# q of batch 1 transposed by DMA from ScalarE's queue in place of TensorE

## The chip, the cores and the metric

The kernel runs on one core of a Trainium2 chip. The metric is the device time of one execution in microseconds, as a median over executions. Engines are named as in the profile: PE is TensorE, ACT is ScalarE, DVE is VectorE, POOL is GpSimd, SP is SyncE, which in this kernel does nothing but issue DMAs.

## The reference, cut to what matters

```python
batch, n_heads, seq, head_dim = 8, 8, 576, 64          # q, k, v, float32
d_model, d_ff = 512, 1024                              # w1, w2: 512x1024; w3: 1024x1024; w_out: 1024x512

def phi(x):
    return np.where(x > 0, x, np.exp(x) - 1.0) + 1.0

q_p, k_p = phi(q), phi(k)
kv = np.einsum('bhsd,bhse->bhde', k_p, v)
z = np.sum(k_p, axis=2)
num = np.einsum('bhsd,bhde->bhse', q_p, kv)
den = np.einsum('bhsd,bhd->bhs', q_p, z)[..., None] + 1e-06
x = (num / den).transpose(0, 2, 1, 3).reshape(4608, 512)

a, b = x @ w1, x @ w2
out = (a * b @ w3) @ w_out
```

## The kernel before

Every step of the program stands in one table, `ORDER`. A step such as `QP.1.0.a` calls the function `s_QP(1, 0)` with engine letter `a` (ACT; `v` is DVE, `s` SP). The steps are recorded in the order of the table, and each engine runs its own instructions strictly in that order; the framework adds the semaphore waits. So a step's place in the table is its place in the queue of every engine that it uses.

Weights come first. `L3`, `LH`, `LO` load w3 and w_out; `T3` transposes w3 on PE, `FW` multiplies it with w_out, so that the second half of the network is one 1024x512 matrix `wf_sb`. `LA`/`CA` and `LB`/`CB` load w1 and w2 in pieces and cast them to bf16.

The attention works by batch b and by half h of the heads (64 sequence rows of two heads share the 128 partitions). `LK`, `LQ`, `LV` load 576 KB each into one of 13 raw buffers. `EX` takes the exponential on ACT (L263), `PT` makes max(x,0)+1 on DVE (L275), and `PM` the minimum of the two on DVE (L282), which is phi. `VC` casts v (L285). `KV` (or `KB`, both halves) makes kv on PE (L298) and copies it out of PSUM.

For the numerator and the denominator PE needs phi(q) with head_dim on the partitions. Two kinds of step do that. `QP` (L322 to L328) transposes nine 128x128 blocks on PE into a PSUM tile `qp` and copies them to SBUF as `qt`; batches 0 and 1 use it. `QD` (L330) is one DMA with transposition from SP, `phq` to `qt`; batches 2 to 7 use it. Then `ND` (one tile of 128 tokens) or `NT`/`NM` (three tiles) multiply `qt` with kv on PE (L344), divide on DVE and write x as `xn`; `XP` on PE or `XD` by DMA transposes that to `xt`.

The network takes chunks of 512 tokens. `F.c.f` makes one of the eight 128-wide column blocks of chunk c: four matmuls into `a_ps`, four into `b_ps` (L428), a copy `a_sb` from `a_ps` by ACT (L437) and a product into `ab` by DVE (L439). `FP` and `FI` are parts of such steps in the first chunk. `O` multiplies with `wf_sb` (L463), `S` stores. The matmul results `a_ps`, `b_ps`, `o_ps`, `xp` take turns in four PSUM buffers, first free first used, so PE's next group waits until the oldest has been copied out.

The program around the change: `FI`, then `F.0.4` to `F.0.7`, with the preparation of batch 1 between them, `KV.1.0` and `KV.1.1`, `O.0`, then `ND.4`, the first step that reads `qt` of batch 1.

DMA completion is told by eight semaphores, `DMAHW0` to `DMAHW7`, handed out in turn in the order of the table, whichever queue the DMA is on. A DMA on SP waits first until the DMA that had its semaphore last has landed, so up to eight are under way.

Of the kernel before, what the change touches and what calls it, by code (L numbers as in the profile page):

```python
# [9 lines left out]
F32 = mybir.dt.float32  # L10
BF16 = mybir.dt.bfloat16
AF = mybir.ActivationFunctionType
ALU = mybir.AluOpType

P = 128
NCH = 512
# [11 lines left out]
PT.k.0.1 T3.7.1.a LH.0.1 FW.7.0.a FW.7.1.v FW.1.2.v VC.0.0.v QP.0.0.v QP.0.1.a FW.7.2.a KV.0.0.a  # L28
PM.k.0.1 VC.0.1.v FW.7.3.v FW.1.3.a KV.0.1.v T3.0.1.a ND.0 FW.0.0.v LA.6 ND.1 FW.0.1.v CA.6.a LA.7
CA.7.a ND.2 FW.0.2.a XP.0.a XP.1.a ND.3 FW.0.3.a FP.0.0.0.0 LB.6 LQ.1.1 EX.q.1.1 LB.7 LA.3 XP.2.v  # L30
XP.3.v FP.0.1.0.0 CB.7.a LA.2 FP.0.1.0.1 LB.3 PT.q.1.1 PM.q.1.1 FI.0.2.0 FI.0.3.0 CB.6.v FI.0.1.1
LB.2 CA.2.a LQ.1.0 CB.3.v FP.0.0.0.1 FI.0.0.1 FI.0.3.1 CB.2.v QP.1.1.v CA.3.a PT.q.1.0 LK.1.0
FI.0.2.1 PT.k.1.0 EX.q.1.0 PM.q.1.0 F.0.4 EX.k.1.0 PM.k.1.0 F.0.5 LV.1.0 VC.1.0.a F.0.6 LK.1.1
EX.k.1.1 PT.k.1.1 PM.k.1.1 LV.1.1 LK.3.0 KV.1.0.a VC.1.1.a F.0.7 LQ.3.1 QP.1.0.a KV.1.1.v PT.k.3.0
EX.q.3.1 EX.k.3.0 O.0.a LQ.3.0 EX.q.3.0 PT.q.3.1 ND.4 ND.5 O.1.a XP.4.a ND.6 ND.7 PM.k.3.0 LK.2.0
XP.5.a O.2.a PM.q.3.1 XP.6.v XP.7.v LQ.2.1 EX.k.2.0 LQ.2.0 PT.k.2.0 PM.k.2.0 PT.q.3.0 EX.q.2.0
LK.3.1 PM.q.3.0 O.3.a LV.4.1 F.1.0 LV.2.0 LK.4.1 S.0.s F.1.1 PT.q.2.1 EX.q.2.1 S.1.s PT.k.3.1 F.1.2
# [26 lines left out]
def kernel(  # L64
# [11 lines left out]
    nc = tc.nc  # L76
    B, H, S, D = q.shape
    DM = H * D
    DFF = moe_w1.shape[1]
    KC = DM // P  # L80
    FC = DFF // P
    R = P // 2
    J = S // R
    HW = 2 * J * D
# [16 lines left out]
    def take(kind, key, shape, dtype, name):  # L101
        if kind in free:
            s = slots[key] = free[kind].popleft()
        else:
            s = taken.get(kind, 0) % turns[kind]
            taken[kind] = taken.get(kind, 0) + 1
        pool = ps if kind in ("mm", "at") else sb
        return pool.tile(shape, dtype, tag=f"{kind}{s}", name=name)

    def give(kind, key):  # L110
        free[kind].append(slots.pop(key))

    ident = consts.tile([P, P], BF16)
    ident32 = consts.tile([P, P], F32)
    zero = consts.tile([P, NCH], BF16)
    w1_sb = wpool.tile([P, KC, DFF], BF16)
    w2_sb = wpool.tile([P, KC, DFF], BF16)
# [5 lines left out]
    def copy_of(e):  # L123
        return {"a": nc.scalar.copy, "v": nc.vector.tensor_copy, "p": nc.gpsimd.tensor_copy}[e]

    def at_tile(name, key=None):
        return take("at", key or name, [P, 2, 512], F32, name)

    def mm_tile(name, key=None):
        return take("mm", key or name, [P, NCH], F32, name)  # L130
# [19 lines left out]
    raw = {}  # L150

    def load(key, src, cols):
        t = raw[key] = take("ld", key, [P, HW], F32, key[0])[:, 0:cols]
        dst = t if len(src.shape) == 2 else t.rearrange("p (a x) -> p a x", a=src.shape[1])
        nc.sync.dma_start(out=dst, in_=src)  # L155

    def head_rows(src, b, h):
        return src[b].rearrange("h (p j) d -> (h p) (j d)", j=J).rearrange(
            "(g p) x -> p g x", p=P)[:, 2 * h:2 * h + 2]
# [4 lines left out]
    def s_LQ(b, h, e):  # L164
        load(("q", b, h), head_rows(q, b, h), HW)

    def s_LV(b, h, e):
        load(("v", b, h), head_rows(v, b, h), HW)

# [89 lines left out]
    es, phs = {}, {}  # L259
# [7 lines left out]
    def by_set(n, t):  # L267

        if n == "k":
            return t.rearrange("p (c j d) -> p c j d", c=2, j=J)  # L270
        return t.rearrange("p (j c d) -> p c j d", c=2, j=J)

    def s_PT(n, b, h, e):
        t = phs[n, b, h] = take("ph" + n, None, [P, HW], BF16, "ph" + n)
        nc.vector.tensor_scalar(out=by_set(n, t), in0=by_set("k", raw[n, b, h]), scalar1=0.0, scalar2=1.0,  # L275
                                op0=ALU.max, op1=ALU.add)
        if (n, b, h) in es:
            give("ld", (n, b, h))

    def s_PM(n, b, h, e):  # L280
        t = by_set(n, phs[n, b, h])
        nc.vector.tensor_tensor(out=t, in0=t, in1=by_set("k", es[n, b, h]), op=ALU.min)  # L282

    def s_VC(b, h, e):
        copy_of(e)(out=vts[b % 2][:, h, :, :, 0:D],  # L285
                   in_=raw["v", b, h].rearrange("p (c j d) -> p c j d", c=2, j=J))
        give("ld", ("v", b, h))


    kvs, qts, xns, xts = {}, {}, {}, {}  # L290
# [27 lines left out]
    def q_tile(b, h):  # L318
        t = qts[b, h] = take("qt", None, [P, J, P], BF16, "qt")
        return t  # L320

    def s_QP(b, h, e):  # L322
# [4 lines left out]
        copy_of(e)(out=t, in_=tp)  # L327
        give("at", "qp")  # L328

    def s_QD(b, h, e):  # L330
        nc.sync.dma_start(out=q_tile(b, h), in_=phs["q", b, h], transpose=True)


    def xn_of(c0):
# [79 lines left out]
    def w_row(kc):  # L414
        return 2 * (kc % 2) + kc // 2

    abs_, ops_, a_sbs, o_sbs = {}, {}, {}, {}


    def f_mm(c0, f, side, tiles=slice(0, CT)):  # L420
        if c0 not in abs_:
            abs_[c0] = take("ab", None, [P, FC, NCH], BF16, "ab")
        key = ("ab"[side], c0, f)
        if key not in ops_:
            ops_[key] = mm_tile("ab"[side] + "_ps", key)
        w = (w1_sb, w2_sb)[side]
        for kc in range(KC):
            nc.tensor.matmul(ops_[key][:, tiles.start * P:tiles.stop * P],  # L428
                             w[:, w_row(kc), f * P:(f + 1) * P], xts[c0][:, tiles, kc, :],
                             start=(kc == 0), stop=(kc == KC - 1))  # L430

    def f_out(c0, f, side):
        key = ("ab"[side], c0, f)
        if side == 0:
            kind = "a_sb" if c0 else "o_sb"
            a_sbs[c0, f] = take(kind, None, [P, NCH], F32, "a_sb" if c0 else "a0_sb")
            nc.scalar.copy(out=a_sbs[c0, f], in_=ops_[key])  # L437
        else:
            nc.vector.tensor_mul(out=abs_[c0][:, f, :], in0=a_sbs[c0, f], in1=ops_[key])  # L439
        give("mm", key)  # L440
# [10 lines left out]
        f_out(c0, f, side)  # L451


    def s_FP(c0, f, side, g, e):
        f_mm(c0, f, side, slice(2 * g, 2 * g + 2))
        if g == 1:
            f_out(c0, f, side)
# [73 lines left out]
```

## Time and profile before

| | us |
|---|---|
| median of 3 runs | 243.34 (243.25 to 243.66) |
| the profiled execution | 241.6 |
| its span, first to last instruction | 239.8 |
| PE busy in the span | 227.6 |
| DVE, ACT, POOL busy | 157.9, 113.9, 1.3 |

Times of the trace count from the start of the span. The profiled execution is 1.7 us shorter than the median, 1.8 us longer than its span. A row of the timeline gives start, length, engine, line, operation, and in brackets how long the engine had sat idle before and what ended that. Instructions of an engine overlap a little in their records: the distance from one start to the next is what an instruction takes of a busy engine.

### The profile page before, as it was taken

Reading aid. Unit: us, or ns where it says so; the run is one execution under the profiler, and the core shown is the slowest. Engines: PE = TensorE matmul, PEld = TensorE weight load, DVE = VectorE, ACT = ScalarE, POOL = GpSimd, SP = SyncE. Lnnn points to the kernel's source line nnn. Section 1 sums busy time; section 2 is a strip of 40 time slices with the busy share of each in tenths; the row PEclk is TensorE's granted clock in tenths of the full one; section 3 lists DMA queues with packets and bytes.
Section 4 is the critical chain, followed back from the end, with each engine's and each line's share of the span. In section 5 each row is a group of like instructions: output and inputs, shape, how many; then the busy total and the mean of one; then the engine's idle time right before and its main releaser. Section 6 shows DMA issues by size and latency. Waiting matters only on the chain.

```text
span 239.8 us, 5452 instructions
## 1 busy us (share of the span) xinstructions
PE 227.6 (95%) x2218; PEld 114.4 (48%) x2237; DVE 157.9 (66%) x287; ACT 113.9 (48%) x166; POOL 1.3 (1%) x9
## 2 busy tenths in 40 slices
PE   1889999999999999999999999999999999999994
PEld 1645665455445444544454445445444444444443
DVE  1278887989998765778865799887663343434131
ACT  3247688798896025946533427542103332133200
POOL 2000000000000000000000000000000000000000
PEclk9999999999999999999999999999999999999999
DMA  6999999999999999999959998995653001700276
GB/s 247 420 382 403 387 386 389 389 392 389 400 278 129 160 347 392 340 190 358 233 108 271 385 362 177 169 202 112 137 121 78 3 0 44 164 13 0 46 155 148
DMA packets 52041, 55.79 MB, mean 233 GB/s; under 512 B 31281, under 2 KB 31537, under 8 KB 52017
## 3 DMA queue, kind: packets, MB, share of 16 engines
q1 hardware_dynamic: 51776, 55.19, 78.7%
q8 instruction: 17, 0.28, 0.5%
q10 hardware_dynamic: 240, 0.26, 0.3%
q14 instruction: 8, 0.06, 0.1%
HBM read 38.80 MB, written 9.44 MB: 201 GB/s over the span
## 4 chain that ended last, share of the span: by engine, by line
PE 92%; DMA 3%; issue 2%; DVE 1%; SPq 1%; ACT 0%; DVEq 0%
PE b_ps L428 26%; PE o_ps L463 26%; PE a_ps L428 26%; PE wf_ps L253 5%; PE nd L344 3%; DMA w<-in_moe_w_dram 3%; PE w3p L241 2%; PE kbp L298 2%; PE qp L326 1%; PE xp L403 1%; PE kvp L298 1%; SPq L155 1%; DVE xt L404 0%; DVE ab L439 0%; DVE w3t L242 0%
## 5 line engine op out<-in xcount | busy, mean ns | idle before, releaser
L428 PEld LDWEIGHTS <-w_sb 128*128 128x128 bf16 x584 | 56.5, 98 | 67.2 <-issue 1.4
L437 ACT COPY a_sb<-a_ps 128x512 f32<-128x512 f32 x72 | 42.2, 587 | 80.4 <-PE a_ps L428 78.5
L439 DVE TENSOR_TENSOR ab<-a_sb,b_ps 128x512 bf16<-128x512 f32 x72 | 49.0, 685 | 38.2 <-PE b_ps L428 36.4
L428 PE MATMUL a_ps<-xt,w_sb 128*128 128x512 bf16 (+1 forms) x296 | 74.0, 373 | 0.1
L428 PE MATMUL b_ps<-xt,w_sb 128*128 128x512 bf16 x288 | 73.8, 379 | 0.1
L463 PE MATMUL o_ps<-wf_sb,ab 128*128 128x512 bf16 (+2 forms) x290 | 63.5, 368 | 1.2 <-issue 0.6
L463 PEld LDWEIGHTS <-ab 128*128 128x128 bf16 x304 | 28.3, 98 | 31.2
L470 DVE COPY o_sb<-o_ps 128x512 f32<-128x512 f32 x23 | 15.8, 689 | 20.7 <-PE o_ps L463 18.9
L350 DVE TENSOR_TENSOR xn<-nd,r 128x512 bf16<-128x512 f32 (+2 forms) x45 | 24.2, 577 | 0.5
L263 ACT ACTIVATE eq<-q 128x1152 bf16<-128x1152 f32 x16 | 18.4, 1164 | 4.8 <-DVE phk L282 3.1
L263 ACT ACTIVATE ek<-k 128x1152 bf16<-128x1152 f32 x16 | 18.7, 1167 | 2.6 <-DMA k<-in_k_dram 2.6
L253 PE MATMUL wf_ps<-wo_sb,w3t 128*128 128x512 bf16 x59 | 16.0, 387 | 2.6 <-DVE wo_sb L207 1.8
L470 ACT COPY o_sb<-o_ps 128x512 f32<-128x512 f32 x12 | 6.9, 581 | 15.0 <-PE o_ps L463 15.0
L275 DVE TENSOR_SCALAR phk<-k 128x1152 bf16<-128x1152 f32 x16 | 12.0, 752 | 1.3 <-DMA k<-in_k_dram 1.3
L282 DVE TENSOR_TENSOR phq<-phq,eq 128x1152 bf16<-128x1152 bf16 x16 | 12.0, 751 | 1.2 <-ACT eq L263 0.5
L241 PE MATMUL w3p<-ident,w 128*128 128x128 f32 x40 | 8.2, 352 | 4.8 <-DMA w<-in_moe_w_dram 4.8
L282 DVE TENSOR_TENSOR phk<-phk,ek 128x1152 bf16<-128x1152 bf16 x16 | 11.9, 751 | 0.2
L275 DVE TENSOR_SCALAR phq<-q 128x1152 bf16<-128x1152 f32 x16 | 12.0, 752 | 0.0
L285 ACT CAST vt<-v 128x1152 bf16<-128x1152 f32 x9 | 10.3, 1160 | 0.0
L241 PEld LDWEIGHTS w3p<-ident,w 128*128 128x128 f32 x40 | 7.0, 214 | 6.4 <-issue 4.7
L253 PEld LDWEIGHTS <-w3t 128*128 128x128 bf16 x64 | 5.6, 98 | 7.1 <-issue 1.5
L344 PEld LDWEIGHTS <-qt 64*64 64x64 bf16 x576 | 6.2, 106 | 4.6 <-issue 3.0
(49 smaller groups left out, 91.1 us busy)
## 6 DMA issues: line engine op xcount, KB each, us to landing
k<-in_k_dram SPq DMA_DIRECT2D x16, 576.0 KB, 9.0
q<-in_q_dram SPq DMA_DIRECT2D x16, 576.0 KB, 9.3
v<-in_v_dram SPq DMA_DIRECT2D x16, 576.0 KB, 7.9
out_dram<-o_sb SPq DMA_DIRECT2D x69, 128.0 KB, 2.7
w<-in_moe_w_dram SPq DMA_DIRECT2D x7, 512.0 KB, 9.5
wo<-in_moe_w_out_dram SPq DMA_DIRECT2D x4, 512.0 KB, 6.7
wa<-in_moe_w_dram SPq DMA_DIRECT2D x4, 512.0 KB, 11.5
wb<-in_moe_w_dram SPq DMA_DIRECT2D x4, 512.0 KB, 11.4
```

What stands on the lines that cost most here:

```text
L241: nc.tensor.transpose(tp[:, c, :], blocks[:, 2 * x + c // 2, c % 2, :], idt)
L253: nc.tensor.matmul(wfs[i], w3ts[i][:, c, :], wo_sb[:, c, :], start=(c == 0), stop=(c == FC - 1))
L263: nc.scalar.activation(out=t, in_=raw[n, b, h], func=AF.Exp)
L275: nc.vector.tensor_scalar(out=by_set(n, t), in0=by_set("k", raw[n, b, h]), scalar1=0.0, scalar2=1.0, op0=ALU.max, op1=ALU.add)
L282: nc.vector.tensor_tensor(out=t, in0=t, in1=by_set("k", es[n, b, h]), op=ALU.min)
L344: nc.tensor.matmul(dst[g * R:(g + 1) * R], qts[b, a // 2][rows, j, a % 2 * R:(a % 2 + 1) * R], kvs[b][rows, a // 2, a % 2, :], start=True, ...
L350: nc.vector.tensor_tensor(out=xn[:, :, a0:a1], in0=n4[:, :, :, 0:D], in1=r.unsqueeze(3).to_broadcast([P, 2, a1 - a0, D]), op=ALU.mult)
L428: nc.tensor.matmul(ops_[key][:, tiles.start * P:tiles.stop * P], w[:, w_row(kc), f * P:(f + 1) * P], xts[c0][:, tiles, kc, :], start=(kc = ...
L437: nc.scalar.copy(out=a_sbs[c0, f], in_=ops_[key])
L439: nc.vector.tensor_mul(out=abs_[c0][:, f, :], in0=a_sbs[c0, f], in1=ops_[key])
L463: nc.tensor.matmul(o_ps, abs_[c0][:, f, m * P:(m + 1) * P], wf_sb[:, f, cols], start=(f == 0), stop=(f == FC - 1))
L470: copy_of(e)(out=o_sbs[t], in_=o_ps)
```

## The change

`QP.1.1.v` and `QP.1.0.a` are taken out and `QD.1.1.a` and `QD.1.0.a` put in. `s_QD` gets a second queue: with the letter `a` the DMA with transposition is issued by ACT. The new steps don't stand where the old ones stood, but directly behind the `PM` steps that write their sources. The diff also adds functions (`s_LS`, `s_ES`, `s_PS`, `s_MS`, `s_QS`, `s_FS`) that no step of the table calls, and letters for POOL that no step uses.

```diff
-XP.3.v FP.0.1.0.0 CB.7.a LA.2 FP.0.1.0.1 LB.3 PT.q.1.1 PM.q.1.1 FI.0.2.0 FI.0.3.0 CB.6.v FI.0.1.1
+XP.3.v FP.0.1.0.0 CB.7.a LA.2 FP.0.1.0.1 LB.3 PT.q.1.1 PM.q.1.1 QD.1.1.a FI.0.2.0 FI.0.3.0 CB.6.v
...
     def s_QD(b, h, e):
-        nc.sync.dma_start(out=q_tile(b, h), in_=phs["q", b, h], transpose=True)
+        (nc.scalar if e == "a" else nc.sync).dma_start(out=q_tile(b, h), in_=phs["q", b, h], transpose=True)
```

ACT's queue in the middle of the first chunk, before; `eq` and `ek` are the exponentials of batch 1, the first `a_sb` copy is that of `F.0.4`, the `qt` copy that of `QP.1.0`:

```order
L263 ACTIVATE eq<-q 128x1152
L437 COPY a_sb<-a_ps 128x512
L263 ACTIVATE ek<-k 128x1152
L437 COPY a_sb<-a_ps 128x512
L285 COPY vt_75<-v 128x18x64
L437 COPY a_sb<-a_ps 128x512
L263 ACTIVATE ek<-k 128x1152
L306 COPY kv<-kvp 128x130
L285 COPY vt_75<-v 128x18x64
L437 COPY a_sb<-a_ps 128x512
L327 COPY qt<-qp 128x1152
```

The same place after:

```order
L271 ACTIVATE eq<-q 128x1152
L383 DMA_TRANSPOSE qt<-phq 128x9x128
L489 COPY a_sb<-a_ps 128x512
L271 ACTIVATE ek<-k 128x1152
L489 COPY a_sb<-a_ps 128x512
L325 COPY vt_75<-v 128x18x64
L489 COPY a_sb<-a_ps 128x512
L271 ACTIVATE ek<-k 128x1152
L346 COPY kv<-kvp 128x130
L325 COPY vt_75<-v 128x18x64
L489 COPY a_sb<-a_ps 128x512
```

The copy `qt` at the end is gone, and the issue of `QD.1.0` stands between the exponential of q and the `a_sb` copy of `F.0.4`, ahead of nine instructions that were ahead of the old one. The issue of `QD.1.1` stands likewise behind the first `a_sb` copy of the chunk, ahead of the second.

DVE at the same place, before, with the semaphores that each row waits for (`DMAHW` is a landing):

```order
L327 COPY qt<-qp 128x1152 [waits PE_49]
L275 TENSOR_SCALAR phq<-q 128x2x9x64 [waits DMAHW4_49]
L439 TENSOR_TENSOR ab<-a_sb,b_ps 128x512 [waits PE_49]
L275 TENSOR_SCALAR phk<-k 128x1152 [waits DMAHW5_49]
L282 TENSOR_TENSOR phq<-phq,eq 128x2x9x64 [waits DVE_49,Activation_49]
```

and after:

```order
L283 TENSOR_SCALAR phq<-q 128x2x9x64 [waits DMAHW5_49]
L491 TENSOR_TENSOR ab<-a_sb,b_ps 128x512 [waits PE_49]
L283 TENSOR_SCALAR phk<-k 128x1152 [waits DMAHW6_49]
L291 TENSOR_TENSOR phq<-phq,eq 128x2x9x64 [waits DVE_49,Activation_49]
L491 TENSOR_TENSOR ab<-a_sb,b_ps 128x512 [waits PE_49,Activation_49]
```

DVE loses the `qt` copy of `QP.1.1`; the rest keeps its order. The last but one row is `PM.q.1.0`, for which `QD.1.0` waits; ahead of it stands `PT.k.1.0`, which waits for the landing of k. The numbers of the landing semaphores have moved by one: the transposition of `QD.1.1` has taken a turn, and that of `QD.1.0` takes another.

More of the change, by code (lines that the diff above doesn't have):

```diff
@@ L30 @@
 CA.7.a ND.2 FW.0.2.a XP.0.a XP.1.a ND.3 FW.0.3.a FP.0.0.0.0 LB.6 LQ.1.1 EX.q.1.1 LB.7 LA.3 XP.2.v
-XP.3.v FP.0.1.0.0 CB.7.a LA.2 FP.0.1.0.1 LB.3 PT.q.1.1 PM.q.1.1 FI.0.2.0 FI.0.3.0 CB.6.v FI.0.1.1
-LB.2 CA.2.a LQ.1.0 CB.3.v FP.0.0.0.1 FI.0.0.1 FI.0.3.1 CB.2.v QP.1.1.v CA.3.a PT.q.1.0 LK.1.0
-FI.0.2.1 PT.k.1.0 EX.q.1.0 PM.q.1.0 F.0.4 EX.k.1.0 PM.k.1.0 F.0.5 LV.1.0 VC.1.0.a F.0.6 LK.1.1
-EX.k.1.1 PT.k.1.1 PM.k.1.1 LV.1.1 LK.3.0 KV.1.0.a VC.1.1.a F.0.7 LQ.3.1 QP.1.0.a KV.1.1.v PT.k.3.0
+XP.3.v FP.0.1.0.0 CB.7.a LA.2 FP.0.1.0.1 LB.3 PT.q.1.1 PM.q.1.1 QD.1.1.a FI.0.2.0 FI.0.3.0 CB.6.v
+FI.0.1.1 LB.2 CA.2.a LQ.1.0 CB.3.v FP.0.0.0.1 FI.0.0.1 FI.0.3.1 CB.2.v CA.3.a PT.q.1.0 LK.1.0
+FI.0.2.1 PT.k.1.0 EX.q.1.0 PM.q.1.0 QD.1.0.a F.0.4 EX.k.1.0 PM.k.1.0 F.0.5 LV.1.0 VC.1.0.a F.0.6
+LK.1.1 EX.k.1.1 PT.k.1.1 PM.k.1.1 LV.1.1 LK.3.0 KV.1.0.a VC.1.1.a F.0.7 LQ.3.1 KV.1.1.v PT.k.3.0
 EX.q.3.1 EX.k.3.0 O.0.a LQ.3.0 EX.q.3.0 PT.q.3.1 ND.4 ND.5 O.1.a XP.4.a ND.6 ND.7 PM.k.3.0 LK.2.0
@@ L165, in s_LQ, with s_LS @@
         load(("q", b, h), head_rows(q, b, h), HW)
+    def s_LS(x, e):
+        src = q[0].rearrange("h (p j) d -> (h p) (j d)", j=J).rearrange("(g p) x -> p g x", p=P)
+        if x == 0:
+            load(("qs", x), src[:, :, 0:4 * D], 4 * 4 * D)
+        else:
+            load(("qs", x), src[:, 2 * x - 2:2 * x, 4 * D:J * D], 2 * (J - 4) * D)
     def s_LV(b, h, e):
@@ L274, in s_PT @@
         t = phs[n, b, h] = take("ph" + n, None, [P, HW], BF16, "ph" + n)
-        nc.vector.tensor_scalar(out=by_set(n, t), in0=by_set("k", raw[n, b, h]), scalar1=0.0, scalar2=1.0,
-                                op0=ALU.max, op1=ALU.add)
+        (nc.gpsimd if e == "p" else nc.vector).tensor_scalar(
+            out=by_set(n, t), in0=by_set("k", raw[n, b, h]), scalar1=0.0, scalar2=1.0,
+            op0=ALU.max, op1=ALU.add)
         if (n, b, h) in es:
@@ L282, in s_PM, with sets_of, qs_in, qs_out @@
         nc.vector.tensor_tensor(out=t, in0=t, in1=by_set("k", es[n, b, h]), op=ALU.min)
+    def sets_of(x):
+        return (range(4), 4) if x == 0 else (range(4, J), 2)
+    def qs_in(x, t):
+        sets, c = sets_of(x)
+        return t[:, 0:c * len(sets) * D].rearrange("p (c j d) -> p c j d", c=c, d=D)
+    def qs_out(x, t):
+        sets, c = sets_of(x)
+        return t[:, 0:c * len(sets) * D].rearrange("p (j c d) -> p c j d", c=c, d=D)
+    def s_ES(x, e):
+        t = es["qs", x] = take("e", None, [P, HW], BF16, "eq")
+        sets, c = sets_of(x)
+        nc.scalar.activation(out=t[:, 0:c * len(sets) * D], in_=raw["qs", x], func=AF.Exp)
+        if ("qs", x) in phs:
+            give("ld", ("qs", x))
+    def s_PS(x, e):
+        t = phs["qs", x] = take("phq", None, [P, HW], BF16, "phq")
+        (nc.gpsimd if e == "p" else nc.vector).tensor_scalar(
+            out=qs_out(x, t), in0=qs_in(x, raw["qs", x]), scalar1=0.0, scalar2=1.0,
+            op0=ALU.max, op1=ALU.add)
+        if ("qs", x) in es:
+            give("ld", ("qs", x))
+    def s_MS(x, e):
+        t = qs_out(x, phs["qs", x])
+        nc.vector.tensor_tensor(out=t, in0=t, in1=qs_in(x, es["qs", x]), op=ALU.min)
     def s_VC(b, h, e):
@@ L328, in s_QP, with s_QS @@
         give("at", "qp")
+    def s_QS(x, h, e):
+        if (0, h) not in qts:
+            q_tile(0, h)
+        sets, c = sets_of(x)
+        n = len(sets)
+        tp = at_tile("qp")[:, 0].bitcast(BF16).rearrange("p (j t) -> p j t", t=P)[:, 0:n]
+        for i in range(n):
+            col = i * c * D + (h * P if x == 0 else 0)
+            nc.tensor.transpose(tp[:, i, :], phs["qs", x][:, col:col + P], ident)
+        copy_of(e)(out=qts[0, h][:, sets[0]:sets[-1] + 1], in_=tp)
+        give("at", "qp")
     def s_QD(b, h, e):
-        nc.sync.dma_start(out=q_tile(b, h), in_=phs["q", b, h], transpose=True)
+        (nc.scalar if e == "a" else nc.sync).dma_start(out=q_tile(b, h), in_=phs["q", b, h], transpose=True)
     def xn_of(c0):
@@ L451, in s_FI, with s_FS @@
         f_out(c0, f, side)
+    def s_FS(c0, f, side, g, e):
+        if c0 not in abs_:
+            abs_[c0] = take("ab", None, [P, FC, NCH], BF16, "ab")
+        cols = slice(2 * g * P, 2 * (g + 1) * P)
+        p = mm_tile("ab"[side] + "_ps")[:, 0:2 * P]
+        w = (w1_sb, w2_sb)[side]
+        for kc in range(KC):
+            nc.tensor.matmul(p, w[:, w_row(kc), f * P:(f + 1) * P], xts[c0][:, 2 * g:2 * g + 2, kc, :],
+                             start=(kc == 0), stop=(kc == KC - 1))
+        if side == 0:
+            if (c0, f) not in a_sbs:
+                a_sbs[c0, f] = take("o_sb", None, [P, NCH], F32, "a0_sb")
+            nc.scalar.copy(out=a_sbs[c0, f][:, cols], in_=p)
+        else:
+            nc.vector.tensor_mul(out=abs_[c0][:, f, cols], in0=a_sbs[c0, f][:, cols], in1=p)
+        give("mm", "ab"[side] + "_ps")
     def s_FP(c0, f, side, g, e):
```

## The prediction

> **What bounds the kernel now.** First the page: which engine fills the span, and of what the chain that ended last is made.
>
> ```profile
> span 239.8 us, 5452 instructions
> PE 227.6 (95%) x2218; PEld 114.4 (48%) x2237; DVE 157.9 (66%) x287; ACT 113.9 (48%) x166; POOL 1.3 (1%) x9
> PE   1889999999999999999999999999999999999994
> ACT  3247688798896025946533427542103332133200
> DMA  6999999999999999999959998995653001700276
> PE 92%; DMA 3%; issue 2%; DVE 1%; SPq 1%; ACT 0%; DVEq 0%
> ```
>
> PE is busy in 95% of the span and makes 92% of the chain. A microsecond taken from PE is a microsecond gained, if nothing else comes late. But this average hides that ACT is nearly full and all DMA engines are full in the eighth and ninth of the forty slices, where batch 1 is prepared. So next the windows there and behind (length, then busy us of PE, PEld, DVE, ACT, POOL, then PE's granted clock, the DMA engines' busy share, GB/s).
>
> ```profile
> 42.00:52.00 10.00, 9.84 (x124) 5.07 (x123) 9.44 (x16) 8.48 (x11) 0.00 (x0) 1.00 1.05 390
> 52.00:60.00 8.00, 7.95 (x109) 4.30 (x108) 7.00 (x18) 7.06 (x11) 0.00 (x0) 1.00 1.05 390
> 60.00:130.00 70.00, 69.47 (x791) 33.23 (x794) 54.45 (x97) 38.17 (x57) 0.00 (x0) 1.00 0.99 266
> 130.00:232.00 102.00, 101.58 (x832) 47.46 (x837) 58.72 (x105) 34.41 (x55) 0.00 (x0) 1.00 0.55 131
> ```
>
> From 52 to 232 us PE is idle for 0.05 + 0.53 + 0.42 = 1.0 us in 180. Nothing behind the change can make up for a delay of PE: what PE loses at 50 us is lost at the end. From 42 to 52 us the DVE has 0.56 us and ACT 1.52 us to spare, and all 16 DMA engines are full. That is where the change sets in.
>
> **What is removed.** The timeline of PE, with its nine-block transpositions `qp`:
>
> ```profile
> 41.60 0.67 PE L326 MATMUL qp<-ident,phq 128*128 128x128 bf16 x9
> 42.10 1.03 PE L428 MATMUL b_ps<-xt,w_sb 128*128 128x512 bf16 x4
> ...
> 46.42 1.03 PE L428 MATMUL a_ps<-xt,w_sb 128*128 128x512 bf16 x4
> ...
> 48.24 0.48 PE L298 MATMUL kvp<-vt,phk 64*64 64x65 bf16 x36
> ...
> 50.40 0.67 PE L326 MATMUL qp<-ident,phq 128*128 128x128 bf16 x9
> 50.99 0.48 PE L298 MATMUL kvp<-vt,phk 64*64 64x65 bf16 x36
> ...
> 53.24 0.45 PE L344 MATMUL nd<-kv,qt 64*64 64x65 bf16 x32
> ```
>
> The two transpositions take PE from 41.60 to 42.10 and from 50.40 to 50.99, together 1.09 us. That is all that the change can win on PE. The copies out of PSUM go too:
>
> ```profile
> 43.01 0.75 DVE L327 COPY qt<-qp 128x1152 bf16<-128x1152 bf16 x1
> 44.94 0.75 DVE L275 TENSOR_SCALAR phk<-k 128x1152 bf16<-128x1152 f32 x1
> 45.61 0.75 DVE L282 TENSOR_TENSOR phq<-phq,eq 128x1152 bf16<-128x1152 bf16 x1
> ...
> 51.10 1.12 ACT L327 COPY qt<-qp 128x1152 bf16<-128x1152 bf16 x1 [0.22 <-PE qp L326]
> ```
>
> DVE saves 0.67 us (the step from 44.94 to 45.61 for an instruction of the same 0.75 us), ACT about 1.1 us, but only at 51.1 us.
>
> **What is added, and where it stands.** Two DMAs with transposition, each with an issue on ACT, a wait of ACT ahead of it, and traffic. The trace has twelve of the same shape, all from SP (nanoseconds: shortest, median, longest), a window of six microseconds in which almost nothing but transpositions ran, and ACT's only issues, three plain stores at the end.
>
> ```profile
> L331 SPq DMA_TRANSPOSE qt<-phq x12: 1281/1350/2352, 68.0 to 159.2; - x12
> DMA to landing us min/median/max: 3.3/3.6/4.5
> ...
> DMA packets 4754, 1.19 MB, mean 198 GB/s; under 512 B 4754, under 2 KB 4754, under 8 KB 4754
> ...
> 235.32 2.13 ACTq L476 DMA_DIRECT2D out_dram<-o_sb  x3
> ```
>
> No row shows ACT issuing a transposition. The bounds: 2.13 / 3 = 0.7 us, ACT's price for a plain store, and 2.35 us, SP's dearest transposition of this shape. I take 1.35 us, the median of the same instruction on the other queue. Traffic: 128 x 1152 x 2 bytes = 0.295 MB at 198 GB/s is 1.5 us of all DMA engines.
>
> **The first one, QD.1.1.** It stands behind the first `a_sb` copy and waits for `PM.q.1.1`, which ended at 37.89.
>
> ```profile
> 37.13 0.76 DVE L282 TENSOR_TENSOR phq<-phq,eq 128x1152 bf16<-128x1152 bf16 x1
> ...
> 37.91 0.59 ACT L437 COPY a_sb<-a_ps 128x512 f32<-128x512 f32 x1 [0.18 <-PE a_ps L428]
> ...
> 43.23 1.16 ACT L263 ACTIVATE eq<-q 128x1152 bf16<-128x1152 f32 x1 [1.49 <-DMA q<-in_q_dram]
> 44.30 0.57 ACT L437 COPY a_sb<-a_ps 128x512 f32<-128x512 f32 x1
> 44.77 1.16 ACT L263 ACTIVATE ek<-k 128x1152 bf16<-128x1152 f32 x1
> 45.83 0.57 ACT L437 COPY a_sb<-a_ps 128x512 f32<-128x512 f32 x1
> 46.30 1.17 ACT L285 CAST vt<-v 128x1152 bf16<-128x1152 f32 x1
> ```
>
> ACT issues from 37.9 to 39.3, and the copies and casts behind it come up to 1.35 us later, until 43.2, where ACT used to stand 1.49 us for q. That wait hides it, so I cost the issue itself at nothing; at 2.35 us about 0.9 us of it would stick out, at a place where PE has the 0.50 us of the removed transposition to spare. Its traffic is not hidden: the DMA engines are full, and the loads of q and k of `LQ.1.0` and `LK.1.0` are already queued.
>
> **The second one, QD.1.0, sets the result.** ACT holds the issue until `PM.q.1.0` is done, and `PM.q.1.0` stands on DVE behind `PT.k.1.0`, which waits for k. SP's timeline with two loads of k (that of `LK.1.0` and that of `LK.3.0`), and the landing time of the first:
>
> ```profile
> 32.91 0.71 SPq L155 DMA_DIRECT2D k<-in_k_dram  x1
> ...
> 39.00 0.99 SPq L155 DMA_DIRECT2D k<-in_k_dram  x1
> ...
> k<-in_k_dram SPq DMA_DIRECT2D x1, 576.0 KB, 11.7
> ```
>
> k lands at 32.91 + 11.7 = 44.6. `QD.1.1` delays it by 0 (its packets queue behind) to 1.5 us (they go first). I take 1.5: the slowest landing of the row above, 4.5 us, puts the transposition in by 42.4, ahead of k. So:
>
> - k lands at 46.1. `PT.k.1.0` 46.1 to 46.8, `PM.q.1.0` to 47.55. (Before, it was done at 45.61 + 0.75 = 46.36, and nobody on ACT waited for it.)
> - ACT issues from 47.6 to 48.95. Until then the `a_sb` copy of `F.0.4` is stuck behind it, which before began at 44.30: 4.65 us late.
> - PE has four PSUM buffers. The `a_ps` of `F.0.6` (46.42) needs the one that this copy empties, so PE stands from 46.4 to 49.5.
> - ACT then does the same row of work as before: from the start of that copy to the end of the cast of v 46.30 + 1.17 - 44.30 = 3.17 us, so the cast ends at 52.1. `KV.1.0` on PE needs it and starts at 52.2 instead of 48.24: 3.95 us late.
> - `KV.1.1` needs the next cast of v. ACT had no idle time there, so it comes about as late: 50.99 becomes 55.0, with the 0.59 us of the second transposition swallowed in the wait. ACT's saved `qt` copy comes only behind this.
>
> From there on PE is 4.0 us late and the windows leave nothing to win it back. Both savings of PE are in this sum already, since they only lengthen its waits. 241.6 + 4.0 = 245.6 for an execution like the profiled one; against the median of the runs, 243.34, the same difference gives 247.3.
>
> Bounds of the sum: k not delayed and an issue of 0.7 us: `PM.q.1.0` done at 44.65 + 0.7 + 0.75 = 46.1, ACT free at 46.8, cast at 50.0, KV at 50.05: 1.8 us, so 245.1. Upper: k 1.5 us later and 2.35 us of issue: 5.0 us. There the landing counts too: 47.6 + 11.7 (the loads' time to landing in these full queues) = 59.3, while `ND.4`, the first reader, would start at 53.24 + 5.0 = 58.2: 1.1 us more, 249.4 in all.
>
> **Two rules beside the rows.** SP's load issue at 32.91 takes 0.71 us. The Trainium skill, "Perfetto Trace Analysis", section "DMA Instruction — HWDGE (DVE, Sync)", says that the descriptor generator is shared between issuing sequencers and locked by one at a time. By that, an issue on ACT could also wait for SP's, an estimate of up to 0.7 us each, and the sum would be 248.0; no row here shows two queues issuing under load. The other concerns landing: the skill's "DMA: Bandwidth & Descriptors", section "Queues, rings and completion order", has each DMA engine take packets in turn from the queues that have work. By that QD.1.1 would be mixed with the loads and delay k by less; with an estimated 1.0 us in place of 1.5 the sum would be 246.8. The trace of before has no such mixture either.
>
> SP's queue: the two DMAs take two of the eight landing semaphores, so SP's load of k for batch 3 waits for QD.1.1. Landed by 42.4 to 49.6 (11.7 us), it would be issued up to 10 us later than at 39.0, but the other semaphores let six loads be queued ahead of it, of 0.59 MB at 390 GB/s = 1.5 us each, nine microseconds of work, so the DMA engines don't run dry by more than a little. I cost it at nothing: the cover is those six loads, and without them batch 3 would come late by what is missing.
>
> **The rivals.**
>
> 1. Longer hold, or a late landing: ACT's issue is pushed back by the full DMA engines beyond SP's 2.35 us, or `ND.4` stands for `qt`. For it: DMA share 1.05 there, and SP's twelve were issued at quieter times. Against: ACT's queue is empty but for these two. From 2.35 us of issue on it decides: 249.4, and each microsecond adds one. Chance 0.21.
> 2. Faster: the hold is short enough. PE loses nothing if the copy of `F.0.4` is done by 46.42, thus if the issue is over by 45.8 and `PM.q.1.0` by 44.5. Then the 1.09 us of PE remain as gain: 242.25. For it: DVE is 0.67 us earlier without its `qt` copy, and ACT might let the later copies pass. Against: k lands only at 44.6 even undelayed, and two DVE steps follow. Chance 0.06.
> 3. A small wait, near the lower bound: 245.1 to 246. Chance 0.08.
> 4. PE's clock falls while it stands: all windows have it at 1.00, but PE stands there for 0.16 us at most in ten, not for 3. If it ran at half speed for as long as it had stood (3.1 us), it would do half of 3.1 us less: 1.55 us on top, 248.9. The skill's "TensorE: Matmul & The Clock Gate", "Part 1: The HAM clock gate", gives half clock after an idle window of about 3.4 us; by it this stand is just short. Chance 0.04.
>
> That the change does nothing is no rival: the order has both DMAs on ACT.
>
> **How the numbers follow.** The forecast, 246 to 248.6, has 0.59; with the rivals 0.98; the last 0.02 are a cancellation. The range 245.0 to 249.8 takes in the forecast, rivals 3 and 4 and about two thirds of rival 1: 0.85. Faster by over 0.2% 0.06, within 0.2% (what a measurement of this kernel can tell from nothing) 0.02, slower 0.92.
>
> **What would show it.** In the profile after: PE idle of 2 to 4 us in front of the `a_ps` of `F.0.6`, released by ACT; ACT idle on DVE's `phq`; two ACTq rows DMA_TRANSPOSE of 1.35 us; the loads of k and q at 44 us landing 1.5 us later; PE's busy time about 1.1 us lower over a longer span. I am wrong if the copy of `F.0.4` starts before 46, if PE's idle time lies before 44 us, at `ND.4` or behind it, or if PE makes up for it after 60 us.

## The result, and the profile after

| | us |
|---|---|
| before, median of 4 runs | 243.50 (243.25 to 243.85) |
| after, median of 4 runs | 246.78 (246.54 to 248.16) |
| ratio after / before | 1.0145, 95% interval 1.0104 to 1.0186 |
| after, profiled execution (span) | 246.55 (244.8) |
| after, repeated later, median of 6 runs | 247.75, ratio 1.0191 (1.0151 to 1.0231) |

The change makes the kernel slower by 3.3 us in the first comparison and 4.3 us in the repetition (against 243.41 us of before, measured beside it); the forecast was +4.0 us. First the page of after.

```profile
span 244.8 us, 5433 instructions
PE 229.6 (94%) x2219; PEld 113.5 (46%) x2219; DVE 157.4 (64%) x286; ACT 112.7 (46%) x165; POOL 1.3 (1%) x9
...
PE   1989999687999999999999999999999999999994
...
DMA  6999999999999979999895999786784001710275
GB/s 254 417 377 405 387 387 387 284 197 390 392 398 246 160 219 360 405 224 344 261 180 163 360 403 199 191 168 118 160 124 93 0 3 24 165 25 3 43 156 144
...
PE 83%; DMA 10%; DVE 3%; issue 1%; SPq 1%; ACT 0%; DVEq 0%
PE o_ps L533 24%; PE b_ps L480 23%; PE a_ps L480 23%; DMA qt<-phq 6%; PE wf_ps L261 5%; DMA w<-in_moe_w_dram 3%; PE nd L396 2%; PE w3p L249 2%; DMA q<-in_q_dram 2%; PE kbp L338 2%; SPq L155 1%; PE xp L455 1%; DVE phq L283 1%; DVE xn L402 1%; PE qp L366 0%
```

The GB/s of before, for comparison:

```profile
GB/s 247 420 382 403 387 386 389 389 392 389 400 278 129 160 347 392 340 190 358 233 108 271 385 362 177 169 202 112 137 121 78 3 0 44 164 13 0 46 155 148
```

PE has lost its nines in the eighth to tenth slices, 43 to 61 us, and only there. In the eighth and ninth, where before had 389 and 392 GB/s, the DMA engines move 284 and 197: the queues that were full ran thin. And the chain holds a new piece, a transposition `qt<-phq` with 6% of the span, followed by a load of q with 2%. PE's timeline shows the waits that opened (the waits are in brackets).

```profile
48.53 1.02 PE L480 MATMUL a_ps<-xt,w_sb 128*128 128x512 bf16 x4 [1.84 <-ACT a_sb L489]
...
51.22 0.48 PE L338 MATMUL kvp<-vt,phk 64*64 64x65 bf16 x36 [0.80 <-ACT vt L325]
...
53.89 0.48 PE L338 MATMUL kvp<-vt,phk 64*64 64x65 bf16 x36 [0.35 <-ACT vt L325]
54.30 1.90 PE L533 MATMUL o_ps<-wf_sb,ab 128*128 128x512 bf16 x8
...
59.38 0.40 PE L455 MATMUL xp<-ident,xn 128*128 128x128 bf16 x4 [0.96 <-DVE xn L402]
...
60.41 0.32 PE L396 MATMUL nd<-kv,qt 64*64 64x65 bf16 x16 [0.39 <-DVE xn L402]
```

There are two groups: three waits for ACT from 46 to 54 us, which the prediction had, and two for DVE's `xn` at 59 to 60 us, which it did not have. The first group has its cause on ACT's timeline.

```profile
38.05 1.35 ACTq L383 DMA_TRANSPOSE qt<-phq  x1
...
42.77 1.19 ACT L271 ACTIVATE eq<-q 128x1152 bf16<-128x1152 f32 x1
46.51 1.35 ACTq L383 DMA_TRANSPOSE qt<-phq  x1
47.90 0.58 ACT L489 COPY a_sb<-a_ps 128x512 f32<-128x512 f32 x1 [3.94 <-issue]
...
57.52 1.16 ACT L271 ACTIVATE eq<-q 128x1152 bf16<-128x1152 f32 x1 [3.21 <-DMA q<-in_q_dram]
```

ACT stands from 43.96 until `PM.q.1.0` is done (DVE's row is 45.72 with 0.76), issues for 1.35 us, and only then copies `a_sb` of `F.0.4`. This stand and issue are called the hold from here on. The second group has its cause in the last row: q of batch 3 lands at 57.5, where before it was there for ACT at 52.16 without any wait:

```profile
52.16 1.16 ACT L263 ACTIVATE eq<-q 128x1152 bf16<-128x1152 f32 x1
```

The chain of waits tells why, and it goes past the hold altogether (start, length, what; `SPq` is SP's queue, `issue` time in which nothing was waited for).

```profile
37.26 0.76 DVE phq L291
38.02 0.03 DVE w_sb L224
38.05 13.53 DMA qt<-phq
51.58 0.02 issue
51.59 0.02 SPq L155
```

SP's own timeline in the same stretch:

```profile
37.08 0.37 SPq L155 DMA_DIRECT2D k<-in_k_dram  x1
39.77 0.37 SPq L155 DMA_DIRECT2D v<-in_v_dram  x1
51.64 0.37 SPq L155 DMA_DIRECT2D k<-in_k_dram  x1
52.10 0.93 SPq L155 DMA_DIRECT2D q<-in_q_dram  x2
```

`QD.1.1` was under way for 13.53 us. It holds the semaphore that SP's `LK.3.0` waits for, and SP issued nothing from 40.1 to 51.6; before, that load went out at 39.00. The queue emptied meanwhile, so q of batch 3, which goes out right behind `LK.3.0`, came 5.4 us late.

That this q decides the time is seen on DVE. Its first step on it, `PT.q.3.1`, stands in DVE's order ahead of the divisions of `ND.4`:

```profile
57.53 0.76 DVE L283 TENSOR_SCALAR phq<-q 128x1152 bf16<-128x1152 f32 x1 [1.31 <-DMA q<-in_q_dram]
...
58.63 0.69 DVE L402 TENSOR_TENSOR xn<-nd,r 128x512 bf16<-128x512 f32 x1
```

The first matmul of chunk 1, `F.1.0`, starts on PE at 64.80, 7.27 us behind the start of that step. The distance is 7.27 or 7.28 us in all five profiles in which DVE stands for this q and PE then for `xn` (both of after and, further down, "only QD.1.1", "QD.1.0 behind the cast" and "QD.1.1 on SP"), whatever PE had lost ahead of it. In both profiles of before, where neither stands, it is 7.86. So in after the end of the stage is set by the late q, and the hold is covered by it.

The following comparisons go by the stage between the first `a_ps` of chunk 0 and the first `a_ps` of chunk 1 (`F.1.0`), because the stage's start wanders: 34.66 us in the first profile of before, 36.26 in a second. Its length doesn't: 25.61 and 25.62 us. Times of the table are from its start, read off PE's rows; "rest" is from `F.1.0` to the end of the span.

| kernel | KV.1.0 | KV.1.1 | ND.4 | F.1.0 | rest | ratio, 95% interval |
|---|---|---|---|---|---|---|
| before | 13.58 | 16.33 | 18.58 | 25.61 | 179.5 | |
| before again | 13.59 | 16.34 | 18.59 | 25.62 | 179.6 | 1.0018 (0.9982 to 1.0055) |
| after | 16.45 | 19.11 | 21.36 | 30.03 | 180.0 | 1.0145 (1.0104 to 1.0186) |
| after again | 16.66 | 19.65 | 21.90 | 29.81 | 180.3 | 1.0191 (1.0151 to 1.0231) |
| only QD.1.0 | 16.46 | 19.12 | 21.37 | 30.85 | 179.5 | 1.0221 (1.0173 to 1.0270) |
| only QD.1.1 | 13.81 | 18.55 | 20.80 | 28.88 | 181.3 | 1.0132 (1.0084 to 1.0179) |
| QD.1.0 behind the cast | 13.59 | 18.06 | 21.98 | 29.89 | 181.2 | 1.0226 (1.0193 to 1.0260) |
| only QD.1.0, behind the cast | 13.59 | 16.10 | 18.35 | 33.19 | 179.9 | 1.0312 (1.0269 to 1.0355) |
| only QD.1.0, behind F.0.4 | 16.03 | 18.70 | 20.95 | 32.54 | 179.6 | 1.0197 (1.0157 to 1.0236) |
| QD.1.0 on SP | 13.58 | 16.04 | 18.29 | 25.75 | 181.1 | 1.0020 (0.9989 to 1.0052) |
| QD.1.1 on SP | 13.30 | 16.05 | 18.30 | 26.18 | 180.0 | 0.9980 (0.9959 to 1.0001) |
| QD.1.1 on SP, later | 13.08 | 15.82 | 18.07 | 25.11 | 180.3 | 1.0007 (0.9978 to 1.0035) |
| both on SP | 13.08 | 15.54 | 17.78 | 27.38 | 180.6 | 1.0154 (1.0110 to 1.0198) |

The first profiled execution of "QD.1.0 on SP" ran at a granted clock of 0.668 and took 346.07 us, where the median is 243.93, so the table has a second set of runs of it.

### The profile page after: what moved, and what is told of

It reads as the page before. It is cut to its first block, busy times and chain, and to the rows that moved or that the text cites. A ratio compares the mean times of both kernels' runs of the same rounds, so it can differ in the third digit from the quotient of the medians.

```text
span 244.8 us, 5433 instructions
## 1 busy us (share of the span) xinstructions
PE 229.6 (94%) x2219; PEld 113.5 (46%) x2219; DVE 157.4 (64%) x286; ACT 112.7 (46%) x165; POOL 1.3 (1%) x9
## 4 chain that ended last, share of the span: by engine, by line
PE 83%; DMA 10%; DVE 3%; issue 1%; SPq 1%; ACT 0%; DVEq 0%
PE o_ps L533 24%; PE b_ps L480 23%; PE a_ps L480 23%; DMA qt<-phq 6%; PE wf_ps L261 5%; DMA w<-in_moe_w_dram 3%; PE nd L396 2%; PE w3p L249 2%; DMA q<-in_q_dram 2%; PE kbp L338 2%; SPq L155 1%; PE xp L455 1%; DVE phq L283 1%; DVE xn L402 1%; PE qp L366 0%
## 5 line engine op out<-in xcount | busy, mean ns | idle before, releaser
L533 PE MATMUL o_ps<-wf_sb,ab 128*128 128x512 bf16 (+2 forms) x304 | 64.9, 369 | 0.0
L261 PE MATMUL wf_ps<-wo_sb,w3t 128*128 128x512 bf16 x64 | 17.2, 390 | 2.2 <-DVE wo_sb L215 1.9
```

The costliest lines, as they stand in the source:

```text
L261: nc.tensor.matmul(wfs[i], w3ts[i][:, c, :], wo_sb[:, c, :], start=(c == 0), stop=(c == FC - 1))
L533: nc.tensor.matmul(o_ps, abs_[c0][:, f, m * P:(m + 1) * P], wf_sb[:, f, cols], start=(f == 0), stop=(f == FC - 1))
```

## The experiments

**Before and after again.** The two kernels were run once more, unchanged, to see how far profiles of the same kernel differ.

> The kernel before, unchanged, for a second trace: its first profiled execution (241.6 us) was 1.7 us shorter than the median of its runs (243.34). If the missing 1.7 us lie in the stage of batch 1, the trace shows F.1.0 at about 62 us instead of 60.3; if they lie elsewhere, the first a_ps of chunk 1 stays at 60.3.

Before ran at 1.0018 of itself, the stage equal to 0.01 us. What differs between two profiles of it, 1.7 us of span, lies ahead of the stage: the profiled execution that the prediction was built on had an early start.

> The change itself, unchanged, with more runs: from the first a_ps of chunk 0 to the first a_ps of chunk 1 the traces give 25.6 us before and 30.0 after, but the medians differ by 3.3 us only. If the stage is the whole story, more runs give 4 to 5 us, ratio 1.016 to 1.021; if the change also starts that stage earlier by about 1 us, the ratio stays at 1.012 to 1.015.

After came to 1.0191, as expected if the stage is the whole story. The stage is 0.2 us shorter than in its first profile. PE waited 2.06 us for `a_sb` and its clock fell behind that (last section), but `F.1.0` follows the late q by 7.27 us as in the first. In both profiles the hold and the late q are there, `QD.1.1` landing 13.5 us after its issue.

**Only the second transposition on ACT.** `QP.1.1` goes back to PE.

```diff
-PM.q.1.1 QD.1.1.a FI.0.2.0
+PM.q.1.1 FI.0.2.0
...
-CB.2.v CA.3.a
+CB.2.v QP.1.1.v CA.3.a
```

> QD.1.0 on ACT as in the change, q of the other half (QP.1.1) on TensorE as before. Theory hold (ACT's queue stands for PM.q.1.0, then issues): KV.1.0 at 51.2 us and F.1.0 about 3 us later than before, the ratio 1.010 to 1.014, nearly the whole loss. Theory dry (SP's loads stand for the landing of QD.1.1 at 51.6 us, the DMA engines run empty, q of batch 3 comes 5.4 us late): with QD.1.1 gone q of batch 3 lands at 52 to 54, and the loss is under half, ratio 1.000 to 1.006.

Up to `ND.4` this is after to 0.02 us: the hold alone makes 2.88 us at `KV.1.0`. But then PE stands a second time (start, length, engine, and the wait in brackets), and the chain shows for what.

```profile
49.14 1.02 PE L480 MATMUL a_ps<-xt,w_sb 128*128 128x512 bf16 x4 [1.84 <-ACT a_sb L489]
...
59.19 0.45 PE L396 MATMUL nd<-kv,qt 64*64 64x65 bf16 x31 [2.23 <-DMA qt<-phq]
```

```profile
47.10 12.04 DMA qt<-phq
59.14 0.04 issue
```

Here SP was not held ahead of the issue, its queue was full, and the transposition took 12.04 us; in after it took 5.9. The ratio, 1.0221, is above both ranges that were expected: dropping this half of the change made it no faster. SP's queue runs dry here too: it issues nothing from 47.99 to 59.20, when its next k had waited for this landing. (That k, `LK.3.1`, is the tenth DMA behind `QD.1.0` in the table; eight semaphores in turn would stop the eighth. Why it is the tenth stays open.)

**Only the first one on ACT.** `QP.1.0` goes back to PE, so ACT isn't held.

```diff
-PM.q.1.0 QD.1.0.a F.0.4
+PM.q.1.0 F.0.4
...
-LQ.3.1 KV.1.1.v
+LQ.3.1 QP.1.0.a KV.1.1.v
```

> QD.1.1 on ACT as in the change, QP.1.0 on TensorE as before. Theory hold: ACT has no wait for DVE in front of F.0.4's copy, so KV.1.0 stays at 48.2 and the ratio is 0.997 to 1.003. Theory dry: SP stands for QD.1.1 until about 50 us, q of batch 3 lands at 56 or later instead of 52, ACT waits 3 to 5 us for it, ratio 1.010 to 1.018.

`KV.1.0` is late by 0.23 us only, so the hold is gone. ACT now waits for one load after the other:

```profile
47.11 1.16 ACT L325 CAST vt<-v 128x1152 bf16<-128x1152 f32 x1 [0.70 <-DMA v<-in_v_dram]
...
50.08 1.16 ACT L271 ACTIVATE ek<-k 128x1152 bf16<-128x1152 f32 x1 [1.33 <-DMA k<-in_k_dram]
...
51.95 1.16 ACT L325 CAST vt<-v 128x1152 bf16<-128x1152 f32 x1 [0.55 <-DMA v<-in_v_dram]
...
56.20 1.16 ACT L271 ACTIVATE eq<-q 128x1152 bf16<-128x1152 f32 x1 [1.60 <-DMA q<-in_q_dram]
```

So the DMA whose semaphore the prediction costed at nothing makes 3.27 us of the stage by itself. The last of these waits, for q of batch 3, sets the end (7.28 us ahead of `F.1.0`). Without `QD.1.0` in the count of semaphores SP stands one load later, at `LQ.3.1`, and this q is there 1.16 us earlier in the stage than in after; the stage is shorter by 1.15. The two losses don't add: 5.24 and 3.27 alone, 4.42 together.

**The hold taken away, the rest kept.** `QD.1.0` is issued behind the cast of v that `KV.1.0` needs.

```diff
-PM.q.1.0 QD.1.0.a F.0.4
+PM.q.1.0 F.0.4
...
-VC.1.0.a F.0.6
+VC.1.0.a QD.1.0.a F.0.6
```

> The change, with QD.1.0's issue moved behind the cast of v (VC.1.0) in ACT's queue; QD.1.1 stays on ACT. Theory hold: the 2.9 us in front of KV.1.0 are gone, F.1.0 comes 1.6 us late (what q of batch 3 added), ratio 1.003 to 1.009. Theory dry: QD.1.1 still lands at about 50 us, SP's loads stand, k and v of batch 1 and q of batch 3 come late as in the run with QD.1.1 alone (3.3 us), ratio 1.010 to 1.016, although nothing on ACT waits for DVE.

The hold is gone (13.59), and hardly anything is gained at `F.1.0`: 29.89, in after 30.03 and 29.81. The ratio is above both ranges that were expected. PE waits 2.15 us for the second cast of v instead, since its load lands late, and the clock falls behind that wait, so the next eight matmuls take 3.57 us. Neither costs anything at the end: `F.1.0` follows the late q by the same 7.27 us. So the hold did not decide the time: with it gone, the late loads set the end of the stage alone.

**The same with only the second transposition.** The last two edits together: no hold and no `QD.1.1`.

> QP.1.1 on TensorE as before; QD.1.0 on ACT, but its issue stands behind the cast of v (VC.1.0) in ACT's queue, where PM.q.1.0 is long done. Theory hold: the wait is gone, KV.1.0 back at 48.2, KV.1.1 about 0.5 us late at most, and if qt lands before ND.4 (53 us) the ratio is 0.997 to 1.004; if it lands 8 us after the issue (57 us) PE waits up to 4 us in front of ND.4 and the ratio is 1.008 to 1.016. Theory dry says the same of the hold and nothing of the landing: 0.997 to 1.003.

The dearest of all, and twice what was expected at most (1.016). Everything up to `ND.4` is on time, then PE stands for `qt`.

```profile
53.69 0.21 PE L396 MATMUL nd<-kv,qt 64*64 64x65 bf16 x1
59.39 0.65 PE L396 MATMUL nd<-kv,qt 64*64 64x65 bf16 x31 [5.49 <-DMA qt<-phq]
59.97 3.59 PE L533 MATMUL o_ps<-wf_sb,ab 128*128 128x512 bf16 x8
```

The issue was at 47.08 and the landing 12.26 us behind it, much as with the hold in place (12.04). The hold had been covering a part of this wait, 5.49 us here and 2.23 there. The clock is at half behind it: the eight matmuls of `o_ps` take 3.59 us, in before 1.90.

**Behind F.0.4.** Only `QD.1.0`, issued one copy later, so that PE's PSUM buffer comes free in time.

```diff
-PM.q.1.0 QD.1.0.a F.0.4 EX.k.1.0
+PM.q.1.0 F.0.4 QD.1.0.a EX.k.1.0
```

> QP.1.1 on TensorE; QD.1.0 on ACT directly behind the a_sb copy of F.0.4 instead of ahead of it. If the copy's PSUM buffer is what makes PE late, F.0.6 starts on time (46.4 us where the first a_ps of the chunk starts at 34.7) and KV.1.0 is late by less than 1 us. If ACT's chain up to the cast of v is what counts, KV.1.0 is still 2 to 2.5 us late, since exponential, copy and cast all wait behind the issue that ends at about 47.9. The landing 12 us after the issue makes ND.4 wait in either case: ratio 1.018 to 1.026.

PE doesn't stand ahead of `F.0.6` any more, but `KV.1.0` is still 2.45 us late, released by the cast:

```profile
51.93 0.48 PE L338 MATMUL kvp<-vt,phk 64*64 64x65 bf16 x36 [2.38 <-ACT vt L325]
...
59.88 0.45 PE L396 MATMUL nd<-kv,qt 64*64 64x65 bf16 x31 [2.82 <-DMA qt<-phq]
```

So the path of the hold is ACT's whole row of work up to the cast, not the PSUM buffer. And `qt` comes late again, 12.2 us after its issue. The ratio, 1.0197, is as expected.

**One transposition on SP.** The same DMA, from the queue that has the loads. First `QD.1.0`, behind the loads that `ND.4` doesn't need:

```diff
-O.0.a LQ.3.0 EX.q.3.0
+O.0.a LQ.3.0 QD.1.0 EX.q.3.0
```

> QP.1.1 on TensorE; QD.1.0 issued by SP behind the load of q (LQ.3.0) instead of by ACT. ACT holds nothing, so KV.1.0 is on time (13.6 us behind the first a_ps). If ACT's queue makes the landing late (packets in turn with SP's loads), the same DMA on SP's queue lands behind the loads ahead of it, at about 55 to 56 us, and ND.4 waits 2 to 3 us: ratio 1.006 to 1.012. If a full DMA makes any transposition late, it lands 12 us after its issue at 46.4, at 58 to 59 us: ratio 1.020 or more.

> The run with QD.1.0 alone on SP once more, for a trace at full clock. Its time (1.005) says that qt lands earlier than the 12 us that ACT's took. In its own turn behind the loads ahead of it: landing at 55 to 56 us and 2 to 3 us of wait in front of ND.4. If ND.4 hardly waits (under 1 us), SP's queue passes the transposition faster than the loads' 11.7 us.

The ratio was 1.0047 (1.0019 to 1.0075) in the first set, just below the 1.006 to 1.012 expected for a landing in its turn, and 1.0020 in the second. There is no hold: `KV.1.1` is 0.3 us earlier than before, `ND.4` waits 0.22 us for `qt`, where 2 to 3 were expected, and `F.1.0` starts 0.1 us late. What PE was spared is lost again by a wait of 1.17 us for a later `qt` at 84 us. Then `QD.1.1`, ahead of `LK.3.0`:

```diff
-LV.1.1 LK.3.0
+LV.1.1 QD.1.1 LK.3.0
```

> QP.1.0 on TensorE; QD.1.1 issued by SP behind the load of v (LV.1.1), where PM.q.1.1 is just done, so neither ACT nor SP waits. PE saves the 0.50 us of QP.1.1 and DVE 0.67 us; the loads of batch 3 come 1.5 us later (one transposition), which ACT's slack may or may not take. If the queue is what hurts in the change: F.1.0 25.1 to 26.1 us behind the first a_ps against 25.6 before, ratio 0.996 to 1.003. If 1.5 us of DMA traffic is enough by itself: F.1.0 at 26.6 or later, ratio above 1.004.

```profile
37.66 0.37 SPq L155 DMA_DIRECT2D v<-in_v_dram  x1
39.00 6.91 SPq L383 DMA_TRANSPOSE qt<-phq  x1
46.00 0.58 SPq L155 DMA_DIRECT2D k<-in_k_dram  x1
```

SP is in this issue for 6.91 us, and the transposition lands in its turn, 11.1 us after the start of the issue. The loads behind it come late, but only so far that ACT waits 1.53 us for the q of batch 3, and `F.1.0` starts 0.6 us late. 0.9980 with an interval up to 1.0001: equal, or faster by a hair. The same DMA issued by ACT gave 1.0132: the queue and the place together make 1.5%, about 3.7 us. A last place for it, behind `LQ.3.1`, so that the q of batch 3 goes ahead:

```diff
-LQ.3.1 KV.1.1.v
+LQ.3.1 QD.1.1 QP.1.0.a KV.1.1.v
```

> QP.1.0 on TensorE; QD.1.1 on SP as in the run that gave 0.998, two loads later, behind LQ.3.1. There ACT waited 1.53 us for q of batch 3, which landed behind the transposition; now q goes ahead. If that wait is what cost the gain: F.1.0 25.1 to 25.6 us behind the first a_ps (26.18 there), ratio 0.993 to 0.998. If the transposition's landing comes due instead (ND.4 waits for qt up to 2 us): 26 to 27, ratio 0.999 to 1.005.

Here the stage gains 0.5 us, just the removed transposition. Ten microseconds later PE gives it back, since the loads behind came later (ACT waits 0.87 us for a q at 61.56 and 1.23 us for a k at 70.13):

```profile
71.82 1.02 PE L480 MATMUL a_ps<-xt,w_sb 128*128 128x512 bf16 x4 [0.28 <-ACT a_sb L489]
73.00 1.02 PE L480 MATMUL b_ps<-xt,w_sb 128*128 128x512 bf16 x4 [0.16 <-DVE ab L491]
```

Counted from the stage's start, chunk 2 starts at 49.57, in the second profile of before at 49.18: the gain is lost, and 0.4 us more. The time is the same, 1.0007, where 0.993 to 0.998 was expected.

**Both on SP.** The first two places on SP together.

> Both transpositions by DMA as in the change, but both issued by SP, QD.1.1 behind LV.1.1 and QD.1.0 behind LQ.3.0. If ACT's queue is what the change pays for, most of the loss goes: ratio 0.998 to 1.006 (the two runs with one of them on SP gave 0.998 and 1.005). If the loss is that of DMA transposition as such, 1.010 or more.

This missed what was expected by far: 1.0154. The chain:

```profile
48.12 9.21 DMA qt<-phq
57.33 0.04 issue
57.38 0.45 PE nd L396 x31
```

`QD.1.1` held SP for 5.78 us, three loads were issued behind it, and `QD.1.0` behind those landed 2.4 us too late for `ND.4`. One transposition fits into the slack of SP's queue here, two do not. None of the versions beats the kernel before by more than can be measured.

## Why the prediction was right, point by point

**The number.** The sum gave +4.0 us for the stage; it measured +4.42 and, in the repetition, +4.19. The medians moved by 3.3 and 4.3 us; 247.3 was forecast, 246.78 and 247.75 measured. That it is slower, and that the hold opens, was foreseen; that the size fits so well is luck. The prediction had the hold as the path that sets the end ("The second one, QD.1.0, sets the result"). As measured the hold left PE 2.8 us late at `ND.4`, not 4.0, and the end of the stage was set by q of batch 3, which came late through `QD.1.1`, a term put at nothing. Two terms were wrong in opposite directions.

**The hold was right in kind, and one term of it too big.** ACT stood for `PM.q.1.0`, the issue took 1.35 us, and ACT's copy of `F.0.4`, PE's wait ahead of `F.0.6`, the cast and `KV.1.0` followed as listed. The mis-sized term is k: taken to land 1.5 us later, it didn't land later at all. `PM.q.1.0` ended 11.71 us after the stage began, 11.70 before. So `KV.1.0` came 2.87 us late instead of 3.95. The packets of after from 38 to 42 us, then from 42 to 46 us (queue, then packets, MB, share of the engines; q1 is SP's queue, q10 ACT's) show why:

```profile
q1 hardware_dynamic: 747, 1.56, 105.4%
```

```profile
q1 hardware_dynamic: 636, 1.37, 100.8%
q10 hardware_dynamic: 603, 0.15, 22.2%
```

For four microseconds after its issue `QD.1.1` moved nothing; then it went nearly packet for packet with the loads, and k was almost in. That agrees with the rule of the Trainium skill, "DMA: Bandwidth & Descriptors", "Queues, rings and completion order", on packets taken in turn. The 1.0 us that the prediction worked out from it was still too much, since the packets came so late. Why they did stays open.

**SP's semaphore: the step that failed.** "I cost it at nothing: the cover is those six loads." The six loads were there, the last of them issued at 39.77. But the landing was put at 42.4 to 49.6, from quiet transpositions and from loads; it came at 51.58, 0.18 us behind the landing of the last load, and the next load then took 3.8 us to land in an empty queue. The cover lasted longer than the nine microseconds reckoned, until 51.40, and the landing that it was to hide came behind its end all the same. This step, not the hold, is on the chain that ended last. It sets the whole 4.42 us of after, and with `QD.1.0` left out it made 3.27. That SP stands for this landing is read from the traces: the next load goes out 0.06 us behind it, and in all four profiles with `QD.1.1` on ACT the load that stands is the eighth DMA behind it in the table. A kernel that frees SP of this semaphore and leaves the rest was not run. The same section of the Trainium skill says that the write of a DMA's semaphore comes after all earlier writes of its DMA engine, of other queues too. A landing just behind the last load would fit this; here it is not told apart from shared packets alone.

**The late landing.** The prediction had it only in the upper bound and in rival 1, 59.3 for a landing 11.7 us after the issue. In after it didn't happen, 52.4, since SP's queue had been emptied by the other DMA. With a full queue it did, in three experiments, 12.0 to 12.3 us.

**The signs, and what else held.** The copy of `F.0.4` at 47.90, ACT's stand and the two issues of 1.35 us came as named; PE's wait in front of `F.0.6` was 1.84 us, just under the 2 to 4 named. The load of k at 44 us didn't land later. PE's busy time was no sign: 227.6 and 229.0 in two profiles of before, 229.6 after. And one of the signs of being wrong came too: PE's waits for `xn`, 1.35 us, lie behind `ND.4`. Behind `F.1.0` PE wins nothing back, as forecast: 180.0 against 179.5 us. `QD.1.1`'s issue didn't delay the exponential at 42.77, but it wasn't free. The second half of `F.0.4` on PE waits 0.16 us for a cast of `w_sb` and starts at 9.16 us of the stage, before at 9.17, although `QP.1.1` is gone; with the same DMA on SP behind `LQ.3.1` PE keeps the 0.5 us. Here it made no difference, as the hold came behind it.

**The rivals.** A longer issue: no, 1.35 us twice, 1.57 in the repetition. Faster: no; where the stage did gain, on SP, it was 0.5 us, later given back. A small wait: no. The falling clock, put at 0.04, was seen in the repetition of after, behind 2.06 us, but not in the first profile, behind 1.84; the late q covered it. The lock of the descriptor generator, from the Trainium skill's "Perfetto Trace Analysis", "DMA Instruction — HWDGE (DVE, Sync)", didn't show: with only `QD.1.0` on ACT, SP issued a load in 0.37 us at 47.62, in the midst of ACT's issue of 1.35 us.

## What to carry to other kernels

A DMA that is put on a second queue is still an instruction of the first one if both share landing semaphores: find who waits for its semaphore, and cover that for the time it takes to land in full queues, not in quiet ones. With the queue of the loads full, a small transfer from another queue landed 12.0 to 13.8 us after its issue, in after 0.18 us behind the last load queued. And take a chain of waits apart by both halves of a change: here one wait hid the other, and each half without its partner cost about as much as the whole. A number that fits doesn't show that the path was right.

## What the runs showed of the hardware beyond this

- **Issue of a transposition.** From ACT 1.32 to 1.57 us, with other DMAs under way. From SP with loads queued 2.6, 4.8, 5.8, 6.9 and 7.2 us, for the same transfer. Why SP's differ wasn't tried.
- **Rate of mixed traffic.** While the rest of a transposition from ACT ran without new loads behind it, the DMA engines moved 101 GB/s from 48 to 50 us in after, and 6 GB/s from 58 to 60 us with only `QD.1.0` on ACT, where q and the transposition landed at 59.0 and 59.14. What they waited for stays open.
- **Clock.** PE's granted clock fell to half behind waits of 2.06 and 2.15 us, and of 2.82 and 5.49 us, but not behind the 2.23 us with only `QD.1.0` on ACT, nor behind the 2.38 us of "behind F.0.4". The windows of "QD.1.0 behind the cast" (PE's clock is the number behind POOL):

```profile
52.00:54.00 2.00, 0.00 (x0) 0.10 (x1) 0.24 (x1) 1.14 (x2) 0.00 (x0) 1.00 0.39 83
54.00:56.00 2.00, 1.93 (x40) 0.96 (x40) 0.89 (x2) 0.50 (x2) 0.00 (x0) 0.62 0.83 214
56.00:58.00 2.00, 2.00 (x9) 0.47 (x7) 0.76 (x1) 0.00 (x0) 0.00 (x0) 0.53 1.04 407
```

The Trainium skill, "TensorE: Matmul & The Clock Gate", "Part 1: The HAM clock gate", has the clock fall after an idle window of about 3.4 us that runs freely. Here the measurement differs: waits of 2.06 and 2.15 us, shorter than such a window, were enough, at times.
